# Scores in back-to-back pairs behind the first output tile, in four chunks of a fused attention and feed-forward kernel

## The chip, the cores and the metric

The kernel runs on one core of a Trainium2 chip. The core has a tensor engine (PE, with PEld for its weight loads), a vector engine (DVE), a scalar engine (ACT), a general engine (POOL) and a queue engine (SP); each works through its own list of instructions in order, and they wait for one another by semaphores. Matmuls write to PSUM, which has eight banks of 512 float32 per partition. The metric is the device time of one execution in microseconds; less is better.

## The reference

Attention with a decay bias, and behind it a gated feed-forward layer on the normalised result. There are 8 sequences, 8 heads, 576 positions and head size 64, so 4608 tokens of width 512; the feed-forward width is 1536.

```python
scores = scale * np.matmul(q, k.transpose(0, 1, 3, 2))
bias = -(cum[:, :, :, None] - cum[:, :, None, :])          # cum: running sum of max(s, 0)
scores = np.where(causal, -1e9, scores + np.minimum(bias, 0.0))
attn = softmax(scores); x = attn @ v                        # to (4608, 512)
xn = x / sqrt(mean(x * x) + 1e-6) * rms_g
g = xn @ w_gate; val = xn @ w_val
out = (g * sigmoid(g) * val) @ w_out
```

## The kernel before

The kernel computes for each block of 128 queries only the scores with its own key block and the one before it (the decay makes the rest vanish), and checks at the end that this and its other shortcuts were allowed; a general version stands behind a flag.

**The feed-forward layer sets the frame.** It runs over nine chunks of 512 tokens, numbered 0 to 8 (`ffn`, L660). In a chunk, twelve blocks of 128 hidden columns each take four matmuls for the gate (`Gp`, L670) and four for the value (`Vp`, L679), all 512 columns wide. ACT makes `T` (tanh) from `Gp` (L673), DVE makes `U` from `T` and `Gp` (L682) and then `Ht` from `U` and `Vp` (L675, the last one L687). After that come four output tiles, each of twelve matmuls into one bank `Op` (L692); ACT copies each bank to `osb` (L697) and a DMA writes it out.

**Attention is threaded into gaps.** After each group of four matmuls `step()` (L599) is called: 36 places in a chunk, which the code counts as `phase()` 1 to 36. Places 1 to 24 lie in the gate and value part, 25 to 27 in the first output tile (27 after its copy), 28 to 30 in the second, 31 to 33 in the third, 34 to 36 in the fourth. At a place a planner, run while the program is written, decides what else is issued: casts, loads, transposes by DMA, and either one **score run** or one **attention-value step**.

- A score run `s_step(b, kb, g)` (L225) is for sequence b, key block kb and four heads (g is 0 or 1; for kb 4 all eight heads). It has four matmuls of 64 rows and 256 columns (eight of 64 columns for kb 4), in pairs that use the two halves of the array at once, one for each parity of the head. Even heads go to one bank, odd ones to another. The pair of banks is `psS`, of which there is one. ACT then takes the exponentials to `E` (L274), half of them in the same place and the other half, through `pending`, at the start of the next place; POOL masks `E` (L283). `E` has eight slots, and each is free again when two attention-value steps have read it.
- An attention-value step `av_step(b, qb, g)` (L292) has eight matmuls of 65 columns (four for qb 0). DVE divides (`rZ` L313, `x_sb` L315). With g = 1 ACT also takes the sum of squares (`Square`, L321), POOL makes the normaliser `al_all` (L328, L331), and three places later DVE scales (L338) and a DMA transposes into `xnT`, from which the gate and value matmuls read.
- `can_s()` (L542) decides whether a score run may go: at least 2, 3 or 4 places after the last one, by how far it is from its due place; a free slot of `E`; its transposed keys and queries in place for five places. `can_av()` (L561) wants the scores five places old.

**Banks.** Four banks with the tag F (`psF()`, L101) serve `Gp`, `Vp` and `Op` in turn. In the compiled kernel a new tile takes the free bank whose last tile was finished with first, where "finished" means that its last reader stands earlier in the program. In the prologue some score runs already use two banks of this kind (`pairF()`, L812).

**Checks on DVE.** At places 25 to 35 DVE also runs `check_mag` (L369) and `check_max` (L375) over the cast keys and queries of later sequences: three rounds of one and two of these in chunk 3 (places 25 to 27, 29 to 31, 33 to 35) and three in chunk 4, where the last sequence is reached.

Of the kernel before, what the change touches and what calls it, by code (L numbers as in the profile page):

```python
# [26 lines left out]
def kernel(  # L27
# [13 lines left out]
    B, H, S, D = q.shape  # L41
# [39 lines left out]
    kqTn = kqT.rearrange("d a w (h n) -> d a w h n", h=HP)  # L81
    kqTx = kqT.rearrange("d a w (c h n) -> d a w c h n", c=NSC, h=HP)
    XB = 2
    KB = 4
    v_sb = mp.tile([128, 2, NSC, H, NV], BF16, name="v_sb")

    NE = 8
# [13 lines left out]
    def psF():  # L101
        return pp.tile([128, DM], FP32, name="psF", tag="F", bufs=4)
# [91 lines left out]
    def tail_step(b):  # L194
        pT = psT()
        nw = 2 if b < XB else 1
        for w in range(nw):
# [14 lines left out]
    eread = {}  # L212
    ecount = [0]
# [8 lines left out]
    def slot_free():  # L222
        return eread.get(ecount[0] % NE, 0) == 0

    def s_step(b, kb, g, pair=None):  # L225

        p = b % 2
        N = (256, 256, 256, 192, 64)[kb]
        W = 64 if kb == 4 else 256
        nj = 4 if kb == 4 else 2  # L230
        e = take_slot((b, kb, g), 2 if kb in (0, 1, 2, 3) else 2)
        if pair is None:
            ps = psS()
            pair = (ps[:, 0, :], ps[:, 1, :])
        heads = []
        for j in range(nj):
            hp = (0 if kb == 4 else 2 * g) + j
            for par in (0, 1):
                rs = slice(par * 64, par * 64 + 64)
                if b < KB:  # L240
                    kT = kqTn[rs, p, 0, hp, kb * 128:kb * 128 + 128]
                else:
                    kT = kqTx[rs, p, 0, kb, hp, :]
                if b < XB:
                    qT = kqTn[rs, p, 1, hp, kb * 128:kb * 128 + N]
                    M = N
                else:
                    qT = kqTx[rs, p, 1, kb, hp, 0:64] if kb == 4 else kqTx[rs, p, 1, kb:kb + 2, hp, :]
                    M = W
                nc.tensor.matmul(  # L250
                    pair[par][:, j * W:j * W + M], lhsT=kT, rhs=qT,
                    start=(j == 0), stop=(j == nj - 1))
                heads.append((2 * hp + par, par, j * W))
        if kb == 4:
            Ev = E[:, e].rearrange("p h (a n) -> p (h a) n", n=128)
            h0, nh, nq = 0, 8, 64
        else:
            Ev = E[:, e]
            h0, nh, nq = 4 * g, 4, 128

        def exps(part):
            for h, par, o in part:
                bh = b * H + h
                parts = [(0, N)]
                if b >= XB and kb == 3:
                    parts = [(0, 128), (128, 192)]
                for n0, n1 in parts:
                    eo = Ev[:, h - h0, n0:n1]
                    ei = pair[par][:, o + n0:o + n1]
                    if b >= XB and (n1 - n0) % 128 == 0:  # L270

                        eo = eo.rearrange("k (a p r) -> k a p r", p=32, r=4)
                        ei = ei.rearrange("k (a r p) -> k a p r", p=32, r=4)
                    nc.scalar.activation(out=eo, in_=ei, func=AF.Exp, scale=0.125,  # L274
                                         bias=biasK[:, kb, bh:bh + 1])

        def second(masked=True):
            exps(heads[nj:])
            if masked:
                mask()  # L280

        def mask():
            nc.gpsimd.affine_select(  # L283
                out=Ev[:, :, 0:nq], in_=Ev[:, :, 0:nq],
                pattern=[[0, nh], [1, nq]], compare_op=ALU.is_ge, fill=0.0, base=0,
                channel_multiplier=-1)

        exps(heads[:nj])
        second.mask = mask
        return second  # L290

# [81 lines left out]
    def check_max(i):  # L373
# [19 lines left out]
    pending = []  # L393
# [3 lines left out]
    def at(*key):  # L397
        return done.get(key, 10 ** 6)
# [19 lines left out]
    def check(b, ws=(1, 0)):  # L418
        t = slot[0] + (8 if b >= KB else 0)

        def when(w):
            if b < 2:
                return slot[0] % 2 and chunk[0] == b
            return phase() >= 25 and slot[0] >= t and (w == 0 or ready(0, "cast", b, 1))
        dve_side.extend((lambda w=w: when(w), f) for w in (ws if b < KB else (0, 1)) for f in (
            lambda w=w: check_mag(b, w), lambda: check_max(0), lambda: check_max(1),
            lambda w=w: done.__setitem__(("check", b, w), slot[0])))

    def phase():

        return slot[0] - first[0]
# [14 lines left out]
    def casts(b):  # L446
# [54 lines left out]
        done["T", b, hp, w] = slot[0]  # L501
        last["T"] = slot[0]

    def do_s(key, pair=None):
        b, kb, g = key
        second = s_step(b, kb, g, pair)
        done["S", b, kb, g] = slot[0]
        if kb == 4:
            done["S", b, 4, 1] = slot[0]
        last["S"] = slot[0]  # L510
        return second
# [30 lines left out]
    def can_s():  # L542
        if not s_seq or not slot_free():
            return False
        b, kb, g = s_seq[0]
        if b == 1 and (phase() < 24 and phase() % 2 == 0 or kb == 4 and at("AV", 1, 3, 1) > slot[0]):
            return False
        due = SLOTS * ((b * S + kb * 128) // DM) - (26 if b == 1 else 18 if b < 4 else 14)
        if slot[0] - last["S"] < (4 if slot[0] < due - 24 else 3 if slot[0] < due else 2):
            return False  # L550
        if b >= XB:
# [47 lines left out]
    def step(bare=False):  # L599

        slot[0] += 1
        while pending:
            pending.pop(0)()
        moved = False
        if scaled[0] < len(x_list):
            b, qb = x_list[scaled[0]]
# [10 lines left out]
        if not moved and x_seq and slot[0] - last["X"] >= 2 and not (  # L617
                scaled[0] < len(x_list) and ready(1, "AV", *x_list[scaled[0]], 1)):
            b, w, c = x_seq[0]
# [11 lines left out]
            run_side(pool_side)  # L631
        run_side(dve_side)
        if can_s():
            pending.append(do_s(s_seq.pop(0)))
            if t_seq and t_seq[0][0] == 1 and can_t():
                do_t(t_seq.pop(0))
            return
# [475 lines left out]
```

## Time and profile before

| what | value |
|---|---|
| median of 3 runs | 373.54 us (372.38 to 373.56) |
| the profiled execution's own time | 373.4 us |
| its span, first to last instruction | 371.5 us, granted clock 0.995 |
| busy: PE, DVE, ACT, POOL | 93%, 75%, 64%, 47% of the span |
| chunk 3, from first gate matmul to the next chunk's | 38.67 us (152.96 to 191.63) |
| chunk 4 | 37.57 us (191.63 to 229.20) |
| chunk 5 | 37.05 us (229.20 to 266.25) |
| chunk 6 | 36.06 us (266.25 to 302.31) |
| chunk 7, which holds no attention | 31.08 us (302.31 to 333.39) |

Busy time of PE is the sum of overlapping matmul spans, so the time that a group of matmuls takes is read from its start to the start of the next group. A few matmul records are missing from the trace (a group of four shows x3), and then the gap belongs to the missing one.

### The profile page before, as it was taken

How to read it: one execution, taken by the hardware profiler on the slowest of the kernel's cores; microseconds unless marked ns; L12 is line 12 of the kernel's file. 1: busy time of each engine (PE TensorE's matmuls, PEld its weight loads, DVE VectorE, ACT ScalarE, POOL GpSimd, SP SyncE). 2: the span in 40 equal slices, each digit the busy share in tenths (PEclk: the TensorE clock that was granted, in tenths of full speed). 3: DMA queues.
4: the chain of work that ended last, by engine and by line, in shares of the span. 5: the costliest groups of instructions: out<-in, count | busy, mean ns of one | idle time of the engine just before them, and what ended most of it. 6: DMA issues, size and time to landing. Idle time of an engine off the chain costs nothing.

```text
span 371.5 us, 6891 instructions
## 1 busy us (share of the span) xinstructions
PE 346.3 (93%) x2312; PEld 162.7 (44%) x2356; DVE 277.1 (75%) x523; ACT 238.7 (64%) x624; POOL 176.4 (47%) x281
## 2 busy tenths in 40 slices
PE   1888999899999999899999999999999999999992
PEld 1553444354444444444444444444444444444441
DVE  6777989499887878788889888885488558827820
ACT  3977687457977597777768776776777644223311
POOL 5968625966757474778837934533222300000000
PEclk9999999999999999999999999999999999999998
DMA  7999999999949499959969974993300230020011
GB/s 231 169 229 233 178 230 193 155 210 209 182 113 120 44 210 126 175 61 212 149 167 206 157 105 118 112 103 53 106 16 15 44 106 3 0 85 30 0 61 62
DMA packets 125627, 46.23 MB, mean 124 GB/s; under 512 B 104912, under 2 KB 120784, under 8 KB 125584
## 3 DMA queue, kind: packets, MB, share of 16 engines
q0 software_dynamic: 59920, 11.80, 42.9%
q1 hardware_dynamic: 53040, 24.33, 32.5%
q10 hardware_dynamic: 12624, 9.59, 10.4%
q8 instruction: 20, 0.33, 0.4%
q14 instruction: 23, 0.19, 0.2%
HBM read 38.16 MB, written 9.44 MB: 128 GB/s over the span
## 4 chain that ended last, share of the span: by engine, by line
PE 61%; DVE 14%; POOL 8%; issue 6%; DMA 5%; ACT 4%; ACTq 0%; POOLq 0%; DVEq 0%
PE psF L692 19%; PE psF L670 17%; PE psF L679 17%; PE psS L250 3%; DVE U L682 3%; DMA kq<-in_q_dram 3%; DVE Ht L675 2%; DVE x_sb L315 2%; POOL v_sb L175 2%; DVE xs_sb L338 2%; ACT E L274 2%; DVE acc L375 2%; POOL E L283 2%; DMA kq<-in_k_dram 1%; POOL kqn L141 1%
## 5 line engine op out<-in xcount | busy, mean ns | idle before, releaser
L274 ACT ACTIVATE E<-psS,biasK 128x256 bf16<-128x256 f32 (+3 forms) x352 | 115.1, 416 | 19.1 <-PE psS L250 18.0
L670 PE MATMUL psF<-xnT,wg_sb 128*128 128x512 bf16 x426 | 110.3, 379 | 2.6 <-DVE Ht L675 0.9
L679 PE MATMUL psF<-xnT,wv_sb 128*128 128x512 bf16 x408 | 109.3, 380 | 1.4
L692 PE MATMUL psF<-wout_sb,Ht 128*128 128x512 bf16 x419 | 100.5, 379 | 0.5 <-issue 0.2
L682 DVE SCALAR_TENSOR_TENSOR U<-T,psF 128x512 bf16<-128x512 f32 x108 | 73.7, 682 | 29.2 <-ACT T L673 29.0
L283 POOL TENSOR_SCALAR_AFFINE_SELECT E<-E 128x512 bf16<-128x512 bf16 x72 | 51.5, 716 | 85.5 <-ACT E L274 85.1
L673 ACT ACTIVATE T<-psF 128x512 f32<-128x512 f32 x108 | 64.6, 598 | 42.8 <-PE psF L670 37.5
L675 DVE TENSOR_TENSOR Ht<-U,psF 128x512 bf16<-128x512 bf16 x99 | 67.7, 683 | 6.6
L670 PEld LDWEIGHTS <-wg_sb 128*128 128x128 bf16 x432 | 38.8, 98 | 47.1 <-issue 8.0
L679 PEld LDWEIGHTS <-wv_sb 128*128 128x128 bf16 x432 | 38.6, 98 | 42.6 <-issue 4.6
L692 PEld LDWEIGHTS <-Ht 128*128 128x128 bf16 x432 | 38.7, 98 | 42.0 <-issue 2.3
L338 DVE SCALAR_TENSOR_TENSOR xs_sb<-x_sb,al_all,g_row 128x512 bf16<-128x512 bf16 (+1 forms) x40 | 31.9, 800 | 16.4 <-POOL al_all L331 14.8
L697 ACT ACTIVATE osb<-psF 128x512 f32<-128x512 f32 x36 | 21.4, 595 | 33.5 <-PE psF L692 30.5
L321 ACT ACTIVATE xs_sb<-x_sb 128x512 bf16<-128x512 bf16 (+1 forms) x36 | 23.0, 641 | 22.3 <-DVE x_sb L315 22.0
L175 POOL DMA_DIRECT2D v_sb<-in_v_dram x40 | 35.5, 888 | 0.3 <-issue 0.2
L375 DVE TENSOR_TENSOR acc<-acc,mag 128x1280 bf16<-128x1280 bf16 x32 | 29.0, 922 | 0.4
L250 PE MATMUL psS<-kqT 64*128 64x256 bf16 (+2 forms) x304 | 26.8, 262 | 1.7 <-ACT E L274 1.1
L306 PEld LDWEIGHTS <-E 128*128 128x128 bf16 x320 | 23.1, 101 | 11.3 <-POOL E L283 0.8
L328 POOL TENSOR_SCALAR al_all<-ss_all 128x1 f32<-128x1 f32 (+1 forms) x40 | 11.1, 278 | 29.8 <-ACT xs_sb L321 24.0
L300 PEld LDWEIGHTS <-E 128*128 128x128 bf16 x256 | 21.2, 101 | 8.1 <-DVE x_sb L315 0.7
L331 POOL TENSOR_TENSOR al_all<-al_all,mhalf 128x1 f32<-128x1 f32 (+1 forms) x40 | 22.3, 557 | 3.3
L141 POOL CAST kqn<-kq 128x512 bf16<-128x512 f32 (+1 forms) x30 | 20.7, 710 | 5.8 <-DMA kq<-in_k_dram 3.7
(94 smaller groups left out, 271.9 us busy)
## 6 DMA issues: line engine op xcount, KB each, us to landing
out_dram<-osb SPq DMA_DIRECT2D x36, 256.0 KB, 2.2
kq<-in_q_dram ACTq DMA_DIRECT2D x6, 1024.0 KB, 6.7
v_sb<-in_v_dram POOLq DMA_DIRECT2D x32, 128.0 KB, 6.0
kq<-in_k_dram ACTq DMA_DIRECT2D x2, 1024.0 KB, 9.3
kqn<-in_k_dram POOLq DMA_DIRECT2D x16, 128.0 KB, 4.8
wg_sb<-in_moe_w_gate_dram POOLq DMA_DIRECT2D x2, 768.0 KB, 10.1
wv_sb<-in_moe_w_val_dram POOLq DMA_DIRECT2D x2, 768.0 KB, 12.5
wout_sb<-in_moe_w_out_dram POOLq DMA_DIRECT2D x1, 1536.0 KB, 14.7
```

The lines of the kernel that those rows point to most:

```text
L175: nc.gpsimd.dma_start(out=v_sb[0:n, b % 2, c, :, 0:64], in_=v[b, :, c * 128:c * 128 + n, :].rearrange("h p d -> p h d"))
L250: nc.tensor.matmul(pair[par][:, j * W:j * W + M], lhsT=kT, rhs=qT, start=(j == 0), stop=(j == nj - 1))
L274: nc.scalar.activation(out=eo, in_=ei, func=AF.Exp, scale=0.125, bias=biasK[:, kb, bh:bh + 1])
L283: nc.gpsimd.affine_select(out=Ev[:, :, 0:nq], in_=Ev[:, :, 0:nq], pattern=[[0, nh], [1, nq]], compare_op=ALU.is_ge, fill=0.0, base=0, chan ...
L338: nc.vector.scalar_tensor_tensor(out=xs_sb[0:n, (b * NSC + qb) % NX, :], in0=x_sb[0:n, (b * NSC + qb) % NX, :], scalar=al_all[0:n, col:col ...
L375: nc.vector.tensor_tensor(out=acc[:, sl], in0=acc[:, sl], in1=mag[:, sl], op=ALU.max)
L670: nc.tensor.matmul(Gp, lhsT=wg_sb[:, cc, fs], rhs=xnT[:, cc, x0:x0 + DM], start=(cc == 0), stop=(cc == CC - 1))
L673: nc.scalar.activation(out=T, in_=Gp, func=AF.Tanh, scale=0.5)
L675: nc.vector.tensor_tensor(out=Ht[:, fb - 1, :], in0=pend[0], in1=pend[1], op=ALU.mult)
L679: nc.tensor.matmul(Vp, lhsT=wv_sb[:, cc, fs], rhs=xnT[:, cc, x0:x0 + DM], start=(cc == 0), stop=(cc == CC - 1))
L682: nc.vector.scalar_tensor_tensor(out=U, in0=T, scalar=1.0, in1=Gp, op0=ALU.add, op1=ALU.mult)
L692: nc.tensor.matmul(Op, lhsT=Ht[:, fb, tb * 128:(tb + 1) * 128], rhs=wout_sb[:, fb, :], start=(fb == 0), stop=(fb == FB - 1))
```

## The change

From chunk 3 on, at places 28 to 33, a score run may be followed at once, in the same place, by a second one. The first uses `psS` as always; the second takes two banks with the tag F and puts off its exponentials: the first half is issued two places later, the second half three places later (the first run's second half is issued one place later, as before). `pending` now holds pairs of a place and a function. In these chunks a single score run that is not within six places of its due place is held back at places 25 to 32, and in chunk 6 the last four score runs are held until they can go as pairs.

```diff
-    def s_step(b, kb, g, pair=None):
+    def s_step(b, kb, g, pair=None, hold=False):
...
-        exps(heads[:nj])
+        def head():
+            exps(heads[:nj])
+        if not hold:
+            head()
+        second.head = head
...
+        if b >= XB and slot[0] < due - HOLD and chunk[0] > 2 and 25 <= phase() <= 32 and not can_pair():
+            return False
+        if chunk[0] == B - 2 and len(s_seq) <= 4 and not can_pair():
+            return False
+        return s_ready(b, kb, g)
+
+    def can_pair():
+
+        if len(s_seq) < 2 or chunk[0] < 3 or not 28 <= phase() <= 33:
+            return False
+        return eread.get((ecount[0] + 1) % NE, 0) == 0 and s_ready(*s_seq[1])
...
-        while pending:
-            pending.pop(0)()
+        while pending and pending[0][0] <= slot[0]:
+            pending.pop(0)[1]()
...
         if can_s():
-            pending.append(do_s(s_seq.pop(0)))
+            pair = can_pair()
+            pending.append((slot[0] + 1, do_s(s_seq.pop(0))))
+            if pair:
+                b, kb, g = s_seq.pop(0)
+                more = do_s((b, kb, g), (psF(), psF()), True)
+                pending.extend([(slot[0] + 2, more.head), (slot[0] + 3, more)])
+                done["S", b, kb, g] = slot[0] + 2
+                last["S"] = slot[0] + 1
```

`XB` is 2, `HOLD` is 6 and `B` is 8. `s_ready` is the last part of the old `can_s`, unchanged.

More of the change, by code (lines that the diff above doesn't have):

```diff
@@ L83 @@
     XB = 2
+    HOLD = 6
     KB = 4
@@ L502, in do_t, with do_s @@
         last["T"] = slot[0]
-    def do_s(key, pair=None):
+    def do_s(key, pair=None, hold=False):
         b, kb, g = key
-        second = s_step(b, kb, g, pair)
+        second = s_step(b, kb, g, pair, hold)
         done["S", b, kb, g] = slot[0]
@@ L550, in can_s, with s_ready @@
             return False
+        if b >= XB and slot[0] < due - HOLD and chunk[0] > 2 and 25 <= phase() <= 32 and not can_pair():
[7 more added lines that the diff above has]
+        return eread.get((ecount[0] + 1) % NE, 0) == 0 and s_ready(*s_seq[1])
+    def s_ready(b, kb, g):
         if b >= XB:
@@ L633, in step @@
         if can_s():
-            pending.append(do_s(s_seq.pop(0)))
+            pair = can_pair()
[6 more added lines that the diff above has]
+                last["S"] = slot[0] + 1
+                if kb == 4:
+                    done["S", b, 4, 1] = slot[0] + 2
             if t_seq and t_seq[0][0] == 1 and can_t():
```

## The prediction

> **What bounds the kernel now.** First the busy line of the page, then the busy time by stretches, one for each of chunks 3 to 7:
>
> ```profile
> PE 346.3 (93%) x2312; PEld 162.7 (44%) x2356; DVE 277.1 (75%) x523; ACT 238.7 (64%) x624; POOL 176.4 (47%) x281
> ```
> ```profile
> 152.96:191.63 38.67, 37.65 (x264) 17.11 (x269) 31.64 (x58) 28.90 (x81) 28.30 (x44) 1.00 1.36 159
> 191.63:229.20 37.57, 37.31 (x265) 16.99 (x269) 33.55 (x65) 27.85 (x78) 22.29 (x36) 1.00 1.25 147
> 229.20:266.25 37.05, 36.79 (x252) 16.63 (x256) 25.67 (x53) 28.07 (x78) 15.16 (x27) 1.00 0.70 92
> 266.25:302.31 36.06, 35.80 (x240) 16.44 (x244) 24.29 (x48) 24.30 (x66) 9.30 (x18) 1.00 0.20 47
> 302.31:333.39 31.08, 30.92 (x142) 14.11 (x144) 20.71 (x35) 11.12 (x22) 0.00 (x0) 1.00 0.10 37
> ```
>
> PE (the second number) fills every chunk. Chunk 7 shows the bare feed-forward: 31.08 us for 144 matmuls, 0.216 each, 0.863 for four. What attention adds is read in the timeline of PE, from start to start:
>
> ```profile
> 181.16 2.75 PE L692 MATMUL psF<-wout_sb,Ht 128*128 128x512 bf16 x12
> 183.85 0.29 PE L250 MATMUL psS<-kqT 64*128 64x64 bf16 x8
> 184.07 1.04 PE L692 MATMUL psF<-wout_sb,Ht 128*128 128x512 bf16 x4
> ...
> 263.10 1.03 PE L692 MATMUL psF<-wout_sb,Ht 128*128 128x512 bf16 x4
> 264.06 0.39 PE L250 MATMUL psS<-kqT 64*128 64x256 bf16 x4
> 264.39 1.04 PE L692 MATMUL psF<-wout_sb,Ht 128*128 128x512 bf16 x4
> 265.26 0.29 PE L306 MATMUL psAV<-v_sb,E 128*128 128x65 bf16 x4
> 265.39 1.02 PE L692 MATMUL psF<-wout_sb,Ht 128*128 128x512 bf16 x4
> 266.25 1.03 PE L670 MATMUL psF<-xnT,wg_sb 128*128 128x512 bf16 x4
> ```
>
> Four matmuls ahead of another group take 0.86 (265.39 to 266.25), ahead of a score run 0.96; the run takes 0.33, the group after it 0.87. So a lone run costs 0.10 + 0.33 + 0.01 = 0.43 us; with 64 columns (kb 4) 0.10 + 0.22 + 0.01 = 0.33. An attention-value step costs 0.24, or 0.13 with four matmuls. Sums: chunk 6 is 31.08 + 6 × 0.43 + 0.33 + 8 × 0.24 + 0.13 = 36.04 against 36.06; chunk 5 comes out at 37.03 against 37.05. Chunk 4 has 0.2 over and chunk 3 has 1.0 over, which is waiting. From chunk 5 on no wait is left, only issue: what a run costs PE is what it costs the kernel.
>
> The 0.1 ahead of a run is visible in the waits as weight loads that cannot run ahead (0.42 each); the other two lines come up below:
>
> ```profile
> PEld L250 <- issue: 28.2, 67, 0.5
> ACT xs_sb L321 <- DVE x_sb L315: 22.0, 21, 2.0
> PE psS L250 <- ACT E L274: 1.1, 3, 0.5
> ```
>
> **The change, part by part.** I followed the planner's rules by hand from the places of before. Every chunk from 3 to 6 gets a pair at place 28 and one at 33: eight pairs. The 35 score runs of these chunks fall as 10, 11, 10, 4 instead of 10, 9, 9, 7. Chunks 0 to 2 don't change.
>
> *What a pair saves.* A second run with no full-height matmul ahead of it needs neither the 0.10 nor the tail. Three runs back to back stand in the prologue:
>
> ```profile
> 19.25 0.61 PE L250 MATMUL psF<-kqT 64*128 64x256 bf16 x4
> 19.64 0.53 PE L250 MATMUL psS<-kqT 64*128 64x192 bf16 x4
> 19.96 0.53 PE L250 MATMUL psF<-kqT 64*128 64x192 bf16 x4
> 20.43 0.40 PE L306 MATMUL psT<-v_sb,E 128*128 128x65 bf16 x4
> ```
>
> The middle one takes 0.32 for two steps of 192 columns, 1.2 columns per ns, at a stage where PE runs at half its later 2.37 columns per ns; nothing is lost between runs. At the later pace 256 columns twice make 0.22. So a second run costs 0.22 instead of 0.43, and for kb 4, with four steps of 0.03, 0.14 instead of 0.33: 6 × 0.21 + 2 × 0.19 = 1.64 us. Bounds: 0.1 a pair less if the second run still starts from empty weights; 0.22 a pair at most, since the columns must be streamed.
>
> In words of the Trainium skill (TensorEngine Tiling (Array Packing), Key Properties) changing the tiling mode drains the array, which would be the 0.10. Another of its pages (TensorE: Matmul & The Clock Gate, The mechanism) says that a weight load overlaps matmuls in flight only where its row group differs. By that each pair of score matmuls would wait for a load, and the second run would be hardly cheaper. By that the sum would be 374.3 (rival 3). The prologue rows speak against it.
>
> *What else goes.* The lone run at place 36 of chunk 3 waits for `psS` (eight matmuls take 1.98 before it at 189.31, not 1.82): 0.16 us, gone, since the pair at 33 takes it. The 0.55 wait of the run at 156.50 lies at place 3 of chunk 3, ahead of the change, and stays. Sum of savings: 1.8.
>
> *What is added: exponentials at the seam.* The number of exponentials is the same, but those of the pair at 33 meet the fourth output tile and the next chunk's first. ACT's order is: copy of tile 3, first run (two halves), the square of the attention-value step at 34, first half of the second run (35), copy of tile 4, second half (36), `T`. Four exponentials take 1.56, so a half 0.78; a copy 0.49 to the next start; a square 0.63. PE's order with the pair's start as 0: 0.55 the pair, 0.87, step at 34 (0.24), 0.86, 0.86 (fourth tile ends, 3.4), step at 36 (0.24), gate 0.86, value at 4.5. Banks: first in is first out by last reader, so the value group (`Vp`) of the next chunk takes the fourth tile's own bank, free when its copy ends; `Gp` and `Vp` of the next block take the pair's two banks. Before, no F bank waited for a score. So the path is the square, half a run, the copy.
>
> - Chunks 5 and 6 (DVE free there): the square starts 1.1 after its step (262.86 to 263.96), at 2.5; half a run to 3.9, copy ends 4.55. `Vp` wants the bank at 4.4: 0.12 each.
> - Chunk 4: the step at 34 has g = 0, no square; the copy ends 4.1: nothing. Here `U` is late next (the square of the step at 36 stands before `T`), about 0.3 us inside the need of the next gate.
> - Chunk 3: DVE runs its checks in front of the divide. Before:
>
> ```profile
> 187.91 0.17 DVE L313 RECIPROCAL rZ<-psT 128x4 f32<-128x4 f32 x1
> 188.12 0.42 DVE L315 TENSOR_TENSOR x_sb<-psT,rZ 128x256 bf16<-128x256 f32 x1
> ```
> ```profile
> 188.58 0.63 ACT L321 ACTIVATE xs_sb<-x_sb 128x512 bf16<-128x512 bf16 x1 [2.01 <-DVE x_sb L315]
> 189.21 0.58 ACT L697 ACTIVATE osb<-psF 128x512 f32<-128x512 f32 x1
> 189.69 1.56 ACT L274 ACTIVATE E<-psS,biasK 128x256 bf16<-128x256 f32 x4
> 191.29 0.60 ACT L697 ACTIVATE osb<-psF 128x512 f32<-128x512 f32 x1
> ```
>
>   That step began on PE at 184.95, and its square came 3.6 later. Now it stands at 34. DVE has 9.1 us of work from 181.6 on (scale 0.7, three `mag` at 0.85 to 1.27, five `max` at 0.8 to 1.1, a divide), and then the step's own divide, 0.55, so the square starts at 191.2; the pair, by the same count of matmuls from 178.76, starts at 187.45, 3.7 earlier; half a run to 5.05, copy ends 5.7. `Vp` wants it at 4.9 (a score run at place 1 of chunk 4 lies before it): 0.8, between 0.25 (`max` at 0.8 throughout) and 1.2.
>
> Together 1.1, bounds 0.5 and 1.7. The runs' own banks are free in time: the pair at 28 needs only DVE's last `U` and `Ht`, the pair at 33 the exponentials of the first pair, done 0.7 us before (4.5 after its start, against 5.2).
>
> *What is moved at no cost.* Three attention-value steps go from chunk 6 to 7, the last to place 6, with their squares (ACT busy 36% there), divides, scales and their transposes on SP: `xnT` of the last tokens is issued at place 9 of chunk 7, needed at chunk 8, 27 places or 23 us later; without that cover each us would count. PE pays 3 × 0.24 there instead of in chunk 6. The mask of each second run comes on POOL two places later; its reader stands seven places behind, some 3 us of cover. In chunk 4 the loads of V and the transposes of sequence 6 on POOL and SP move by a place or two, and stand ten places ahead of their readers. Score runs at places 1 and 4 of chunk 4 meet a late ACT: `psS` would be free just when the second wants it (at 8.6), like the 0.5 us wait in the list; inside the bounds.
>
> **Sum.** 373.4 − 1.8 + 1.1 = 372.7 us, against the profiled execution's own 373.4 (0.14 below the median).
>
> **Rivals.**
> 1. *The seam is hidden.* If the squares or copies come 0.3 earlier, or `max` at its short row, only 0.3 is given back: 373.4 − 1.5 to − 1.8, some 371.8. For it: chunks 4 to 6 are within 0.15 of it. Against: chunk 3's DVE queue, 90% busy from 181 to 190.
> 2. *The seam costs more than the pairs save.* One mechanism: the square of place 34 holds ACT at the end of all four chunks as in chunk 3. 4 × 0.85 = 3.4: 375.0. It decides from 0.77 a seam. For it: squares came 2.3 (225.81 to 228.14) and 3.6 us after their steps in chunks 3 and 4. Against: in chunks 5 and 6 they came at 1.1, and chunk 4 has none there.
> 3. *The second run isn't cheaper.* Saving 0.16 alone, give-back 1.1: 374.3. Against: the prologue rows.
>
> The Trainium skill (TensorEngine Tiling (Array Packing), PSUM Bottleneck) also says that tiling speeds up the matmuls, not the evacuation of PSUM; that is rival 2 in kind, and chunk 3's rows bear it out, those of 5 and 6 not.
>
> **How the numbers follow.** Forecast 0.45, rival 1 0.27, rival 2 0.18, rival 3 0.06, others 0.04. A measurement of this kernel tells 0.3% (1.1 us) from no change: faster is under 372.4, slower over 374.7. The forecast's own range, 371.9 to 373.3 by its bounds, puts a third in faster: 0.15, and with rival 1's 0.26 faster is 0.41. Rival 2 gives slower 0.16, rivals 3 and others 0.03: 0.19. Same has 0.40. The range goes from 371.5 (all saved, 373.4 − 1.85) to 374.6 (rival 3's upper side) and leaves out rival 2.
>
> **What would show it.** Right: at eight places a row of L250 into `psS` followed by one into `psF` 0.22 to 0.24 later, and one of them per chunk followed by the feed-forward; chunks 5 and 6 (with 10 and 4 runs) free of waits but 0.1; the first value group of chunk 4 waiting some 0.8 on `osb`. Wrong: a gap of 0.1 or more between the two runs (rival 3), or a wait of L679 on `osb`, or of L670 on `E`, over 0.77 at each seam (rival 2). The forecast falls if the hand-followed places are wrong, above all if fewer than eight pairs form, or if a new wait shows inside a chunk, at the score runs of places 1 to 4.

## The result, and the profile after

The change makes the kernel slower: 377.37 us median of 4 runs (376.71 to 377.46), against 373.31 for the kernel before beside it, a ratio of 1.0113 (95% interval 1.0094 to 1.0131). The profiled execution took 377.41 us, its span 375.6. The forecast was 372.7 with a range to 374.6.

The busy line of the page after, and the busy time by stretches, one for each of chunks 3 to 7 (from, to, length; then busy time and instructions of PE, PEld, DVE, ACT and POOL; clock, DMA share, GB/s):

```profile
PE 346.1 (92%) x2312; PEld 164.0 (44%) x2356; DVE 278.7 (74%) x523; ACT 236.4 (63%) x624; POOL 176.6 (47%) x281
```
```profile
152.23:190.80 38.57, 37.43 (x263) 17.29 (x269) 32.47 (x57) 27.82 (x78) 27.24 (x43) 1.00 1.35 154
190.80:232.12 41.32, 38.02 (x281) 17.66 (x283) 34.07 (x66) 29.84 (x85) 25.87 (x39) 1.00 1.06 132
232.12:270.63 38.51, 37.28 (x268) 17.32 (x270) 26.92 (x56) 29.87 (x84) 15.82 (x28) 1.00 0.68 98
270.63:304.24 33.61, 33.12 (x199) 15.56 (x199) 19.53 (x34) 17.29 (x46) 4.01 (x9) 1.00 0.13 40
304.24:337.49 33.25, 32.41 (x171) 14.80 (x171) 23.51 (x45) 13.12 (x33) 2.68 (x6) 1.00 0.14 42
```

No engine's share of the span rose. What is new is the distance between a chunk's length and PE's busy time in it: 3.3 us in chunk 4, where it was 0.3, 1.2 in chunk 5 (before 0.3), 0.8 in chunk 7 (before 0.2). Chunks 3 to 7 take 185.26 us instead of 180.43.

Three places in the timeline of PE (start, duration, instruction; in brackets the idle time and its releaser): the pair at place 33 of chunk 3 with the seam behind it (the end of one chunk and the first groups of the next), and two waits inside chunk 4.

```profile
187.17 0.39 PE L251 MATMUL psS<-kqT 64*128 64x256 bf16 x4
187.40 0.38 PE L251 MATMUL psF<-kqT 64*128 64x256 bf16 x4
187.72 1.04 PE L719 MATMUL psF<-wout_sb,Ht 128*128 128x512 bf16 x4
...
191.76 0.39 PE L251 MATMUL psS<-kqT 64*128 64x256 bf16 x4
193.40 0.81 PE L706 MATMUL psF<-xnT,wv_sb 128*128 128x512 bf16 x3 [1.24 <-ACT osb L724]
...
211.26 0.20 PE L311 MATMUL psT<-v_sb,E 128*128 128x65 bf16 x1 [0.81 <-POOL E L284]
...
218.29 1.02 PE L706 MATMUL psF<-xnT,wv_sb 128*128 128x512 bf16 x4 [0.79 <-DVE Ht L702]
```

The second run starts 0.23 us after the first, and the output group 0.32 after that: the pair does what it was to do. The value group at 193.40 comes 1.64 after the score run, where 0.33 is normal. Measured like this, from start to start against the same step without a wait, the new waits are:

| where | waits for | us |
|---|---|---|
| chunk 3, first output tile | last `Ht` (DVE) | 0.36 |
| seam 3 to 4, first value group | copy `osb` (ACT) | 1.31 |
| chunk 4, attention-value step at place 17 | mask of `E` (POOL) | 0.97 |
| chunk 4, a value group about place 24 | `Ht` (DVE) | 0.95 |
| seam 4 to 5, first value group | copy `osb` (ACT) | 0.94 |
| chunk 5, a score run | exponentials (ACT) | 0.25 |
| chunk 6, a gate group | `U` (DVE) | 0.33 |
| seam 6 to 7, first value group | copy | 0.13 |
| chunk 7, three groups | `Ht`, `U`, `U` (DVE) | 1.10 |

That is 6.3 us, 2.4 at the seams and 4.0 inside the chunks. Less the 1.8 that the pairs and the lost wait at place 36 save, and with 0.1 more at place 3 of chunk 3 (0.74, before 0.62), it makes 4.7 of the 4.83 found. The span rose by less, 4.1 (375.6, before 371.5), since the stretch ahead of chunk 3 was 0.73 shorter in this execution. Most of that lies ahead of chunk 1, a stretch that takes 72.9 to 75.3 us in the traces here, and so the experiments are read by the lengths of chunks 3 to 7.

### The profile page after: what moved, and what is told of

The parts are those of the page before. It is cut to its first block, busy times and chain, and to the rows that moved or that the text cites. A ratio compares the mean times of both kernels' runs of the same rounds, so it can differ in the third digit from the quotient of the medians.

```text
span 375.6 us, 6882 instructions
## 1 busy us (share of the span) xinstructions
PE 346.1 (92%) x2312; PEld 164.0 (44%) x2356; DVE 278.7 (74%) x523; ACT 236.4 (63%) x624; POOL 176.6 (47%) x281
## 3 DMA queue, kind: packets, MB, share of 16 engines
q1 hardware_dynamic: 53040, 24.33, 31.9%
## 5 line engine op out<-in xcount | busy, mean ns | idle before, releaser
L275 ACT ACTIVATE E<-psS,biasK 128x256 bf16<-128x256 f32 (+3 forms) x308 | 100.7, 421 | 8.5 <-PE psS L251 7.3
L719 PE MATMUL psF<-wout_sb,Ht 128*128 128x512 bf16 x416 | 99.4, 379 | 1.2 <-issue 0.5
L284 POOL TENSOR_SCALAR_AFFINE_SELECT E<-E 128x512 bf16<-128x512 bf16 x72 | 53.0, 736 | 91.9 <-ACT E L275 90.8
L343 DVE SCALAR_TENSOR_TENSOR xs_sb<-x_sb,al_all,g_row 128x512 bf16<-128x512 bf16 (+1 forms) x40 | 32.6, 816 | 9.9 <-POOL al_all L336 8.3
L380 DVE TENSOR_TENSOR acc<-acc,mag 128x1280 bf16<-128x1280 bf16 x32 | 30.2, 958 | 0.3
L251 PE MATMUL psS<-kqT 64*128 64x256 bf16 (+2 forms) x264 | 23.9, 265 | 1.8 <-ACT E L275 1.4
L251 PEld LDWEIGHTS <-kqT 64*128 64x128 bf16 x320 | 11.1, 97 | 26.7 <-issue 24.3
```

The source lines that it names most:

```text
L251: nc.tensor.matmul(pair[par][:, j * W:j * W + M], lhsT=kT, rhs=qT, start=(j == 0), stop=(j == nj - 1))
L284: nc.gpsimd.affine_select(out=Ev[:, :, 0:nq], in_=Ev[:, :, 0:nq], pattern=[[0, nh], [1, nq]], compare_op=ALU.is_ge, fill=0.0, base=0, chan ...
L343: nc.vector.scalar_tensor_tensor(out=xs_sb[0:n, (b * NSC + qb) % NX, :], in0=x_sb[0:n, (b * NSC + qb) % NX, :], scalar=al_all[0:n, col:col ...
L380: nc.vector.tensor_tensor(out=acc[:, sl], in0=acc[:, sl], in1=mag[:, sl], op=ALU.max)
L719: nc.tensor.matmul(Op, lhsT=Ht[:, fb, tb * 128:(tb + 1) * 128], rhs=wout_sb[:, fb, :], start=(fb == 0), stop=(fb == FB - 1))
```

## The experiments

The lengths of the chunks, from first gate matmul to the next chunk's, in us:

| kernel | 3 | 4 | 5 | 6 | 7 |
|---|---|---|---|---|---|
| before | 38.67 | 37.57 | 37.05 | 36.06 | 31.08 |
| after | 38.57 | 41.32 | 38.52 | 33.60 | 33.26 |
| pairs of chunk 3 alone | 38.71 | 42.13 | 37.59 | 35.64 | 31.08 |
| of chunk 4 alone | 38.76 | 37.46 | 37.30 | 35.50 | 31.08 |
| of chunk 5 alone | 38.93 | 37.56 | 36.93 | 35.76 | 31.08 |
| of chunk 6 alone | 39.36 | 37.56 | 37.05 | 34.91 | 33.24 |
| chunk 3, pair at 28 alone | 38.48 | 39.44 | 37.05 | 36.06 | 31.08 |
| chunk 3, no score run at places 1, 2 of chunk 4 | 38.47 | 39.53 | 37.05 | 36.06 | 31.08 |
| chunk 3, without checks | 38.67 | 39.47 | 37.05 | 35.64 | 31.08 |
| chunk 3, loads of V earlier | 38.72 | 40.12 | 37.05 | 35.64 | 31.08 |
| the same, step of 13 at 15 | 38.82 | 40.39 | 37.32 | 35.64 | 31.08 |
| the same as the last but one, casts later | 38.67 | 40.38 | 37.59 | 35.64 | 31.08 |
| chunks 4 to 6, decay checks later | 39.21 | 37.44 | 37.31 | 34.31 | 33.17 |
| chunk 6, odd places in chunk 7 | 38.98 | 37.56 | 37.05 | 34.91 | 32.26 |
| chunks 4 to 6, odd places in chunk 7 | 39.39 | 37.45 | 37.31 | 34.32 | 31.94 |
| all pairs, three causes removed | 38.07 | 38.68 | 37.30 | 33.60 | 32.26 |
| the same, step of 13 at 15 | 38.68 | 38.83 | 37.30 | 33.60 | 32.26 |
| all pairs, casts later as well | 37.84 | 37.99 | 37.29 | 33.60 | 32.28 |

Chunk 3 is the one that varies between executions, by the waits that a score run meets at its place 3 (0 to 1.0 us) and, where no pair stands at 33, at place 36 (0 to 0.65); the kernels are compared by chunks 4 to 7.

### Which chunk's pairs cost

Four kernels, each with the pairs of one chunk alone, here chunk 4; for chunks 3 and 5 the list holds their number, and for chunk 6 the two lines with `B - 2` stay as well.

```diff
-        if b >= XB and slot[0] < due - HOLD and chunk[0] > 2 and 25 <= phase() <= 32 and not can_pair():
-            return False
-        if chunk[0] == B - 2 and len(s_seq) <= 4 and not can_pair():
+        if b >= XB and slot[0] < due - HOLD and chunk[0] in (4,) and 25 <= phase() <= 32 and not can_pair():
             return False
...
-        if len(s_seq) < 2 or chunk[0] < 3 or not 28 <= phase() <= 33:
+        if len(s_seq) < 2 or chunk[0] not in (4,) or not 28 <= phase() <= 33:
```

> Pairs and the hold in chunk 3 alone (places 28 and 33); later chunks take single runs again, four places apart, but two places earlier in chunk 4 than before. Theory Q (the loss is queues: ACT at the end of a chunk, POOL and DVE in chunk 4 because the attention places moved by two against casts and loads, and the decay checks in chunk 7): two pairs save 0.4, the last Ht in the first output tile costs 0.36, the seam to chunk 4 1.3, the POOL and DVE waits inside chunk 4 about 1.9: 3.2 us slower than before. Theory B (each pair keeps two of four F banks, and each chunk with pairs loses alike, a quarter of the 4.1): 1.0 slower, inside chunk 3 and its seam, and chunk 4 keeps its own time.

> Pairs and the hold in chunk 4 alone; chunk 3 and chunk 4 up to place 22 stand as before. Theory Q: two pairs save 0.4, the seam to chunk 5 costs 0.9, no wait inside chunk 4 before place 24: 0.5 us slower than before. Theory B: 1.0 slower.

> Pairs and the hold in chunk 5 alone, where DVE has no more checks of keys and queries. Theory Q: two pairs save 0.4, no seam: 0.4 us faster than before (chunk 5 or 6 shorter by that), at most 0.1 of it lost at the seam. Theory B: 1.0 slower.

> Pairs in chunk 6 alone, with the hold of the last four runs, which sends three attention-value steps into chunk 7 beside the decay checks. Theory Q: two pairs save 0.4, the seam to chunk 7 costs 0.1, chunk 7 loses 1.1 beyond the 0.7 that the three steps take there instead of in chunk 6: 0.8 us slower. Theory B: 1.0 slower, at the seam, and chunk 7 loses nothing inside.

Measured: chunk 3 alone 376.77 us, a ratio of 1.0094 (1.0072 to 1.0117); chunk 4 alone 0.9995 (0.9978 to 1.0011); chunk 5 alone 0.9992 (0.9979 to 1.0005); chunk 6 alone 1.0045 (1.0030 to 1.0061). Chunks 4 to 7 sum to 141.76 before and to 141.34 and 141.33 with the pairs of chunk 4 or 5: 0.42 and 0.43 less, two pairs at 0.21, with no new wait. This is read from one trace each; the medians cannot tell so little. So the pairs save what was forecast where nothing is in their way, and theory B, by which each chunk with pairs loses alike, falls; the seam of 0.9 that theory Q expected behind chunk 4 did not come either. The loss has two sources: the pairs of chunk 3, by what they do to chunk 4 (four waits of 1.20, 0.99, 0.95 and 1.06 there and 0.53 in chunk 5), and those of chunk 6, by what they do to chunk 7 (0.12, 0.28, 0.50 and 0.32). In chunks 4 to 7 the four kernels differ from the kernel before by +4.68, -0.42, -0.43 and +1.00, together +4.83, and the changed kernel by +4.94: the four nearly add up.

### The seam behind chunk 3

Three kernels with chunk 3's pairs: only the pair at place 28; both, with the first score run of chunk 4 held until place 3; and both, without DVE's checks of sequences 5 to 7 (that part is not computed). The edits are shown against the kernel with the pairs of chunk 3 alone.

```diff
-        if len(s_seq) < 2 or chunk[0] not in (3,) or not 28 <= phase() <= 33:
+        if len(s_seq) < 2 or chunk[0] not in (3,) or not 28 <= phase() <= 30:
```
```diff
+        if chunk[0] == 4 and phase() < 3:
+            return False
         return s_ready(b, kb, g)
```
```diff
-            lambda w=w: check_mag(b, w), lambda: check_max(0), lambda: check_max(1),
+            (lambda w=w: check_mag(b, w)) if b < 5 else (lambda: None), (lambda: check_max(0)) if b < 5 else (lambda: None), (lambda: check_max(1)) if b < 5 else (lambda: None),
```

> Chunk 3 alone, with the pair at place 28 but not the one at 33: the runs of sequence 5 go singly at 33 and 36, and chunk 4 keeps the places of before. Theory Q (seam, then POOL and DVE in chunk 4 at moved places): no wait for the fourth tile's copy and none inside chunk 4; left are one pair's 0.2 saved and the 0.36 wait for the last Ht: within 0.4 us of before, chunk 4 at 37.6. Theory H (the hold at place 25 and the pair at 28, by what they shift in ACT and DVE, already bring the loss): most of the 4.7 that chunks 3 to 7 of the run with both pairs lost is still there.

> Chunk 3 alone with both pairs, but no score run at places 1 and 2 of chunk 4, so that the runs of chunk 4 stand at 3, 6, 10, 14, ... as in the kernel before, while the loads of keys and the casts stay two places earlier and the loads of V two later than in it. Theory M (the waits of 1.0 and 0.95 inside chunk 4 come from the attention places that moved by two): they go; left are the seam, 1.2 to 1.7, and 0.36: 1.2 to 1.7 us slower than before. Theory L (they come from loads and casts that crowd POOL at places 9 to 17, wherever attention stands): they stay, 3 us slower or more.

> Chunk 3 alone with both pairs, and the check of keys and queries of sequences 5 to 7 on DVE left out (that part is not computed). Theory D (the seam is late because DVE's checks stand before the divide, which the square, and with it ACT's order, waits for): the wait of 1.2 at the first value group of chunk 4 falls under 0.3, and the 1.06 of the score run at the end of chunk 4 goes too; the two waits inside chunk 4 stay, about 1.9. Theory X (ACT has too many exponentials at the seam, whatever DVE does): the seam stays at 1.0 or more.

Measured: 1.0033 (1.0012 to 1.0053), 1.0058 (1.0038 to 1.0078) and 1.0030 (1.0015 to 1.0045). Without the pair at 33 the seam has no wait, but a score run at place 3 of chunk 4 waits 0.81 for the exponentials, and the mask is late by 0.95 all the same. Chunks 4 to 7 lose 1.87, where theory Q expected next to nothing and theory H most of the 4.7: the pair at 28 and the hold bring a part of the loss by themselves. With the score run held, the value group waits 1.62 instead of 1.20, since nothing stands ahead of it; but inside chunk 4 the wait for the mask is gone and that for `Ht` falls from 0.95 to 0.49. So these two waits hang on the places of attention's runs and steps, as theory M said, the one for `Ht` in part. Without the checks the seam closes, in the timeline of PE:

```profile
191.31 1.03 PE L695 MATMUL psF<-xnT,wg_sb 128*128 128x512 bf16 x4
192.27 0.39 PE L251 MATMUL psS<-kqT 64*128 64x256 bf16 x4
192.60 1.04 PE L704 MATMUL psF<-xnT,wv_sb 128*128 128x512 bf16 x4
```

The value group comes 0.33 after the run; the waits at the end of chunk 4 (1.06, 0.53) are gone as well. So the seam is DVE's checks ahead of the divide, which hold back the square on ACT, the exponentials and the copy behind it. The changed kernel shows this chain in the timelines of DVE and ACT:

```profile
188.83 0.83 DVE L374 TENSOR_SCALAR mag<-kqn 128x2560 uint16<-128x2560 uint16 x1
189.69 1.13 DVE L380 TENSOR_TENSOR acc<-acc,mag 128x1280 bf16<-128x1280 bf16 x1
190.74 0.17 DVE L318 RECIPROCAL rZ<-psT 128x4 f32<-128x4 f32 x1
190.95 0.42 DVE L320 TENSOR_TENSOR x_sb<-psT,rZ 128x256 bf16<-128x256 f32 x1
```
```profile
191.41 0.63 ACT L326 ACTIVATE xs_sb<-x_sb 128x512 bf16<-128x512 bf16 x1 [2.07 <-DVE x_sb L320]
191.94 0.19 ACT L326 ACTIVATION_READ_ACCUMULATOR xs_sb<-x_sb 128x1 f32 x1
...
192.04 0.82 ACT L275 ACTIVATE E<-psF,biasK 128x256 bf16<-128x256 f32 x2
192.75 0.59 ACT L724 ACTIVATE osb<-psF 128x512 f32<-128x512 f32 x1
```

The step began on PE at 188.59, its square 2.8 later. The two waits inside chunk 4 (0.68 for the mask, 0.95 for `Ht`) stay without the checks.

### The waits inside chunk 4

First, with the pairs of chunk 3 alone, the five loads of V that POOL issues, moved to places 5 to 13 (in the changed kernel 9 to 17, before 7 to 15).

```diff
-            (early if b else later)(v_side, 6 if b else 16, [
+            (early if b else later)(v_side, 3 if b == 4 else 6 if b else 16, [
```

> The pairs of chunk 3 alone, and the five loads of V of sequence 6 on POOL at places 5, 7, 9, 11 and 13 of chunk 4 instead of 9 to 17. In the run with chunk 3's pairs alone the attention-value step of place 17 waited 0.99 us for POOL's mask and the value group after it 0.95 for Ht (chunk 4 took 42.13 us). Theory of the crowded POOL: casts (0.6 us each), loads of V (0.9) and sums over partitions (0.75) fall together in places 11 to 15 and make the mask late. Then both waits go, together from 1.94 to under 0.5, and chunk 4 takes 40.5 to 40.8 us; the waits at its two seams (1.18 and 1.06) stay. Rival, the waits come from the exponentials, shifted late by the seam: they stay at 1.6 or more together, and chunk 4 stays at 41.8 to 42.3. Second rival, the crowd only moves to places 5 to 9, where the casts of the K rows start: a new wait of 0.5 or more ahead of place 12.

Measured: 1.0053 (1.0027 to 1.0080). The wait for `Ht` is gone. In the changed kernel DVE's scale waited for POOL's `al_all`, which stood behind a load (215.25 to 215.95), and the `Ht` that PE wanted stood behind the scale:

```profile
216.89 0.75 DVE L343 SCALAR_TENSOR_TENSOR xs_sb<-x_sb,al_all,g_row 128x512 bf16<-128x512 bf16 x1 [1.66 <-POOL al_all L336]
217.56 0.68 DVE L702 TENSOR_TENSOR Ht<-U,psF 128x512 bf16<-128x512 bf16 x1
```

With the loads out of the way it does not. The wait for the mask stays at 0.99. So the theory was right for one of the two. Chunk 4, at 40.12, is shorter than the 40.5 to 40.8 expected, since the 1.06 at its end is gone too.

Next, for the mask, two further kernels on top of this one: the attention-value step of place 13 put to 15, and the casts of sequence 7 put from places 11 to 15 to 14 to 18.

```diff
+        if chunk[0] == 4 and phase() in (13, 14):
+            return False
```
```diff
-        pool_side.extend((lambda w=w: ready(7, "raw", b, w) and free(w), f) for w, f in fns)
+        pool_side.extend((lambda w=w: ready(7, "raw", b, w) and free(w) and not (b == 7 and chunk[0] == 4 and phase() < 14), f)
+                         for w, f in fns)
```

> The pairs of chunk 3 alone, the loads of V at places 5 to 13, and in chunk 4 no attention-value step at place 13 (it goes to place 15). Without this the steps stand at 5, 7, 9, 11 and 13, five of them two places apart, where the kernel before has 7, 9, 11 and 15; the step of place 17 waited 0.99 us for POOL's mask. Theory of the full row: each step gives DVE a divide (0.55) and every second one a scale (0.75) in front of the next U, so that the divide ahead of the square of the step at 13 comes late, ACT waits for it 1.35 us, and with it the exponentials and the mask. Then the wait of place 17 falls from 0.99 to 0.0 to 0.3, and chunk 4 takes 39.1 to 39.5 us instead of 40.12. Rival, POOL's casts in front of the mask alone: the wait stays at 0.8 or more and chunk 4 at 39.9 to 40.2.

> The pairs of chunk 3 alone, loads of V at places 5 to 13, and the five casts of sequence 7 on POOL at places 14 to 18 instead of 11 to 15, so that the two that stood in front of the late mask (0.64 and 0.60 us) now stand behind it. The theory of the full row has fallen: with the step of place 13 moved to 15 the wait of place 17 stayed at 0.99. Theory of POOL's queue in front of the mask (POOL runs without a gap from place 5 to 17, and two casts, a sum over partitions and three loads lie between the mask before and this one): the mask comes 1.2 us earlier, the wait of 0.99 goes to under 0.1, and chunk 4 takes 39.0 to 39.3 us instead of 40.12, of which 1.2 is the seam. Rival, the mask then waits for the exponentials, made late on ACT: the wait stays at 0.4 or more.

Measured: with the step moved the wait stays at 0.99 (374.38 us, one run), and that theory falls: the square on ACT still waits 1.35 for its divide, and the last exponential ahead of the mask still ends 18.2 us after the chunk's start (18.1 without the move), so it is not the step of place 13 that makes it late. With the casts moved the wait is gone (376.8 us in one run, which is read by its chunks). So POOL's queue is what PE waits for. The timeline of POOL in the changed kernel ahead of the mask that PE waits for at place 17:

```profile
204.58 1.07 POOL L284 TENSOR_SCALAR_AFFINE_SELECT E<-E 128x512 bf16<-128x512 bf16 x1 [0.18 <-ACT E L275]
205.60 0.89 POOL L176 DMA_DIRECT2D v_sb<-in_v_dram  x1
206.49 0.69 POOL L156 DMA_DIRECT2D kqn<-in_k_dram  x1
207.17 0.89 POOL L176 DMA_DIRECT2D v_sb<-in_v_dram  x1
208.04 0.63 POOL L150 CAST kqn<-kq 128x512 bf16<-128x512 f32 x1
208.76 0.19 POOL L333 TENSOR_SCALAR al_all<-ss_all 128x1 f32<-128x1 f32 x1
209.03 0.56 POOL L336 TENSOR_TENSOR al_all<-al_all,mhalf 128x1 f32<-128x1 f32 x1
209.56 0.60 POOL L150 CAST kqn<-kq 128x512 bf16<-128x512 f32 x1
210.12 1.08 POOL L284 TENSOR_SCALAR_AFFINE_SELECT E<-E 128x512 bf16<-128x512 bf16 x1
```

From the load at 205.60 on POOL works without a gap of over 0.1 us; the last exponential that this mask needs ended at 209.0. In the kernel before, the same stretch, and the step on PE that reads the mask:

```profile
205.57 0.68 POOL L283 TENSOR_SCALAR_AFFINE_SELECT E<-E 128x512 bf16<-128x512 bf16 x1
...
210.70 0.66 POOL L283 TENSOR_SCALAR_AFFINE_SELECT E<-E 128x512 bf16<-128x512 bf16 x1
```
```profile
211.56 0.19 PE L300 MATMUL psT<-v_sb,E 128*128 128x65 bf16 x1
```

There the mask ended at 211.36, 0.20 us ahead of its reader: the cover of this mask (the time from the end of a result to the start of its reader) was 0.2, not microseconds. The exponentials have their part too: the last one ended 2.7 us after the start of its score run before, and 4.3 after it now. With the casts moved the mask begins right behind it (210.54, the exponential ended at 210.47) and still ends only 0.06 ahead of its reader; no run took this part away alone. And both masks take 0.4 longer now (1.07 and 1.08 instead of 0.68 and 0.66), 0.8 together; why, the last section says.

With the casts later chunk 4 is nevertheless 40.38 us, not 39.0 to 39.3, because the waits of 1.08 and 0.53 at its end, absent with the loads of V moved alone, are back. Two rows in each of the two kernels show what differs. With the loads of V alone, DVE and then POOL, and DVE's next check:

```profile
220.61 0.82 DVE L374 TENSOR_SCALAR mag<-kqn 128x2560 uint16<-128x2560 uint16 x1
...
224.83 0.82 DVE L374 TENSOR_SCALAR mag<-kqn 128x2560 uint16<-128x2560 uint16 x1
```
```profile
221.33 0.66 POOL L284 TENSOR_SCALAR_AFFINE_SELECT E<-E 128x512 bf16<-128x512 bf16 x1 [2.89 <-ACT E L275]
...
225.28 0.86 POOL L284 TENSOR_SCALAR_AFFINE_SELECT E<-E 128x512 bf16<-128x512 bf16 x1 [1.16 <-ACT E L275]
```

With the casts later as well:

```profile
221.17 1.31 DVE L374 TENSOR_SCALAR mag<-kqn 128x2560 uint16<-128x2560 uint16 x1
...
225.89 1.26 DVE L374 TENSOR_SCALAR mag<-kqn 128x2560 uint16<-128x2560 uint16 x1
```
```profile
221.15 0.66 POOL L284 TENSOR_SCALAR_AFFINE_SELECT E<-E 128x512 bf16<-128x512 bf16 x1 [3.01 <-ACT E L275]
...
225.81 0.66 POOL L284 TENSOR_SCALAR_AFFINE_SELECT E<-E 128x512 bf16<-128x512 bf16 x1 [0.62 <-ACT E L275]
```

Where the mask comes first by 0.02 or 0.08 us, the check takes 0.44 to 0.49 longer, twice; where the check comes first, it takes 0.82. The divide behind them is 0.85 later against the chunk's start, and the square waits 3.50 us for it instead of 1.98. The kernel with chunk 3's pairs and no other edit, which has both waits, shows the same: there the mask comes 0.02 and 0.08 ahead, and the checks take 1.31 and 1.26. No run changes this order and nothing else, so that it brings the two waits is argued from three traces.

### Chunk 7

With the pairs of chunks 4 to 6, the checks of the decay, which share DVE with the steps there, were put behind place 16. Then, with the pairs of chunk 6 alone, the three attention-value steps that end up in chunk 7 were put to the odd places 3, 5 and 7 instead of 2, 4 and 6.

```diff
-        dve_side.extend((lambda: chunk[0] == B - 1 and slot[0] % 2, f) for f in [
+        dve_side.extend((lambda: chunk[0] == B - 1 and phase() > 16 and slot[0] % 2, f) for f in [
```
```diff
+        if chunk[0] == B - 1 and phase() % 2 == 0:
+            return False
```

> Pairs in chunks 4, 5 and 6 but not in 3, and the decay checks of chunk 7 moved from its first places to those after 16. By theory Q six pairs save 1.2, the seams cost 0.1 to 0.3 together and chunk 7 loses nothing beyond the three steps that it takes over: chunks 4 to 7 make 140.8 us instead of 141.8, and the whole is 0.9 us faster than before. If the decay checks were not what the steps in chunk 7 met, its 1.2 stay, and the time is that of before.

> The pairs of chunk 6 alone; in chunk 7 the three attention-value steps stand at odd places, behind a gate group, and not at 2, 4 and 6. Theory of the ring: at an even place the transfer T of the next block stands behind the square on ACT, the square behind the divide on DVE, the divide behind U, and U behind T, so that each step adds a wait; at an odd place T is ahead of the square. Then chunk 7 takes 31.08 + 3 x 0.24 + 0.1 (the seam) = 31.9 us, instead of 33.24 with the steps at even places, and the sum of chunks 3 to 7 falls by 1.3. Rival, any attention-value step in chunk 7 costs a wait, as its DVE is short of time: chunk 7 stays at 32.9 to 33.4.

Measured: with the decay checks moved chunk 7 stays at 33.17 (1.0039; 1.0009 to 1.0068): they are not the cause. At odd places it falls from 33.24 to 32.26, and the kernel from 1.0045 to 0.9991 (0.9970 to 1.0012), with one wait of 0.29 left; the forecast was 31.9. That wait goes when the checks of the decay stand behind place 16 as well: 31.94 in the first kernel of the next section. This points to 0.3 us for them at odd places; that kernel has the pairs of chunks 4 and 5 too. The ring (engines that wait for one another in turn) is to be seen in the first of the two kernels, where the decay checks are out of the way, in the timelines of ACT, DVE and PE:

```profile
310.03 0.63 ACT L326 ACTIVATE xs_sb<-x_sb 64x512 bf16<-64x512 bf16 x1 [2.66 <-DVE x_sb L320]
...
310.66 1.05 ACT L700 ACTIVATE T<-psF 128x512 f32<-128x512 f32 x2
```
```profile
311.26 0.69 DVE L709 SCALAR_TENSOR_TENSOR U<-T,psF 128x512 bf16<-128x512 f32 x1 [0.67 <-ACT T L700]
```
```profile
312.00 1.02 PE L697 MATMUL psF<-xnT,wg_sb 128*128 128x512 bf16 x4 [0.34 <-DVE U L709]
```

At an even place, behind a value group, the next block's `T` stands behind the square on ACT; the square waits for the divide, and DVE's `U` for `T`. At an odd place `T` stands ahead of the square, as ACT's timeline of the second kernel shows:

```profile
307.67 0.60 ACT L702 ACTIVATE T<-psF 128x512 f32<-128x512 f32 x1 [0.25 <-PE psF L699]
309.97 0.63 ACT L326 ACTIVATE xs_sb<-x_sb 64x512 bf16<-64x512 bf16 x1 [1.71 <-DVE x_sb L320]
```

Before, the steps with a square in the gate and value part of chunks 4 to 6 all stood at odd places. In the changed kernel the 0.33 in chunk 6 follows two steps at its places 2 and 4, with the same order on ACT (the square at 274.00, `T` at 274.63); no run put these at odd places.

### All together

The pairs of chunks 4 to 6 with both edits of chunk 7; the whole change with the causes found so far removed (checks left out, loads of V earlier, odd places); this with the step of place 13 moved; and this with the casts later instead.

> Pairs in chunks 4, 5 and 6, none in chunk 3; in chunk 7 the attention-value steps at odd places and the checks of the decay after place 16. By the theory (chunk 3's pair and chunk 7's even places are the whole loss) chunks 4 and 5 keep 37.4 and 37.3, chunk 6 takes 33.9 to 34.3 and chunk 7 31.9: 140.5 to 140.9 us against 141.76 in the kernel before, so 0.9 to 1.3 us faster, a ratio of 0.9965 to 0.9976. Rival, the ring also stands at odd places: chunk 7 at 33.2, and the kernel no faster than before.

> The whole change, with the three suspected causes taken away at once: the checks of sequences 5 to 7 on DVE (the three of the magnitude and the maximum) are left out, so that part isn't computed; the loads of V of sequence 6 stand at places 5 to 13 of chunk 4; the attention-value steps of chunk 7 stand at odd places. If these causes are all, chunks 3 to 7 take 179.0 to 180.0 us, against 180.43 before and 185.27 with the change as it stands, and the kernel is 0.4 to 1.4 us faster than before. If something else costs as well, the sum stays above 181.5 and the kernel is slower than before.

> The whole change with the three causes taken away as before (the checks of sequences 5 to 7 on DVE left out, so that part isn't computed; the loads of V at places 5 to 13; odd places in chunk 7) and no attention-value step at place 13 of chunk 4. By the theory of the full row the 0.68 us wait left in chunk 4 falls under 0.2 and chunk 4 takes 38.0 to 38.2 us instead of 38.68: all of chunk 4's loss is then accounted for. By the rival it stays at 38.6 to 38.8.

> The whole change with all causes taken away: the checks of sequences 5 to 7 on DVE left out (not computed), loads of V at places 5 to 13, casts of sequence 7 at places 14 to 18, odd places in chunk 7. By the theory of POOL's queue the 0.68 us left in chunk 4 goes, chunk 4 takes 38.0 to 38.1 us (48 score matmuls and 88 attention-value matmuls with nothing waiting), chunks 3 to 7 take 179.0 to 179.8 us, and the kernel is 0.6 to 1.4 us faster than before, a ratio of 0.996 to 0.9985. By the rival chunk 4 stays at 38.4 to 38.7.

Measured: the first takes 372.20 us, 0.9972 (0.9959 to 0.9984): a version that computes everything and beats both kernels, with a ratio as forecast; its chunks 4 to 7 sum to 141.0, just over the 140.5 to 140.9 forecast, against 141.76 before. The second: 0.9987 (0.9971 to 1.0003), chunks 3 to 7 at 179.9 as forecast, 0.68 left for the mask. The third keeps that wait at 0.67. The fourth: 0.9952 (0.9935 to 0.9969), with chunk 4 as PE's work alone, by the stretches 3 to 5 of this kernel:

```profile
153.83:191.66 37.83, 37.62 (x268) 17.18 (x269) 24.39 (x49) 28.62 (x82) 26.95 (x44) 1.00 1.37 154
191.66:229.65 37.99, 37.99 (x286) 17.52 (x283) 27.81 (x57) 30.31 (x85) 24.18 (x39) 1.00 1.31 151
229.65:266.94 37.29, 37.29 (x273) 17.21 (x271) 24.82 (x51) 28.56 (x80) 14.96 (x27) 1.00 0.66 93
```

Chunk 4 takes 37.99, 3.33 less than in the changed kernel, with no wait left. Chunks 3 to 7 sum to 179.0, 1.43 under the kernel before, with 1.1 of waits still in them (0.36, 0.33, 0.13, 0.30). Of the 1.43, 0.83 is chunk 3, whose wait at place 3 is absent in this execution; chunks 4 to 7 sum to 141.16, 0.60 under the kernel before. This kernel lacks the checks, which the kernel before has, and the kernel before was not run without them. So it is no version to use, and the 0.60 is no clean measure of the pairs; it shows that the loss goes when these causes are taken away.

## Why the prediction was wrong

- **The pairs** (places 28 and 33 of chunks 3 to 6, runs 10, 11, 10, 4): right.
- **What a pair saves:** right. The second run starts 0.23 us after the first in all eight pairs, and two pairs save 0.42 and 0.43 where they stand alone. Rival 3 falls, and with it the rule on weight loads that the prediction set beside it: in the pair at 187.17 the second run's first weight loads begin at 187.40, while the first run's last matmuls (187.29 to 187.56) are in flight. On this kernel a second run costs its columns. The 0.16 at place 36 went too.
- **The seams:** mechanism right, size off. Forecast 0.8, 0, 0.12, 0.12 (1.04, entered as 1.1); measured 1.31, 0.94, 0, 0.13. At chunk 3 the value group wanted its bank 4.92 us after the pair's start, as counted (4.9), but the square came at 4.24 instead of 3.7 and the copy ended at 6.17 instead of 5.7. DVE's work ahead of the divide took 9.8 us where 9.1 was counted (the scale 1.23 for 0.7, and three of the maxima 1.13, 1.19 and 1.27, above the counted 0.8 to 1.1), so that the step's own divide began when counted (190.7) although the scale began 0.6 earlier, while the pair stood 0.3 earlier than counted. At chunk 4 the forecast was 0, and the pairs of chunk 4 alone do give 0: the 0.94 comes with chunk 3's pairs, and a wait at the same end (1.06 there) goes when DVE's checks are left out. Rival 2 named the mechanism, but all seams together cost 2.4, not 3.4, and it does not account for the time.
- **"What is moved at no cost":** this is the step that failed. It priced at nothing the moves of chunk 4 and chunk 7, beyond the PE time of the three steps. They cost 0.97 + 0.95 and 1.10, and with 0.25 in chunk 5 and 0.33 in chunk 6 come to 3.6 us, twice what the pairs save. Each of its covers was wrong in the same way: it was measured as places between a result and its reader, not as the idle time of the queue that makes the result. "Its reader stands seven places behind" is true of the paired runs' masks, but a lone run's mask in chunk 4 had 0.20 us in hand before, with POOL full. The loads of V had ten places to their reader, but stand in POOL's queue ahead of masks and sums. And the three steps in chunk 7 were costed as PE time, ACT being busy 36%, although the order on ACT, not its share, sets the ring.
- **Not counted at all:** the score run that the hold takes from place 25 had covered the last `Ht` ahead of the first output tile; without it PE waits 0.36 in chunk 3.

## What to carry to other kernels

Moving work within an in-order schedule is priced on each queue that it passes: look in the trace for the time between the end of a result and the start of its reader there, since a full queue may leave a cover of tenths of a microsecond however many places lie between, as POOL's did here (0.2). Where steps of different engines alternate, ask behind which half a step lands, for the order may close a ring at one place and not at the next. Test a change that stands in several stages one stage at a time: here two of the four were free and the other two made the loss.

## What was unexpected of the hardware

POOL's mask takes 0.63 to 0.68 us alone, or beside DVE's `Ht`, `U` and divide; in the changed kernel all twelve masks that took over 1.0 us (1.04 to 1.83) overlap DVE's scale (L343) or a check (L374, L380). It works both ways: the check took 0.82 when it came first and 1.31 when the mask did. The Trainium skill (SBUF — State Buffer, Who interferes with whom) says that a vector instruction with two SBUF inputs, or in a two-port mode, shuts POOL out and the reverse, by which was issued first; the trace agrees, since the scale and the maximum read two tensors in SBUF, while `Ht` and `U` read one there and one in PSUM and leave the mask at 0.63. Of the check L374, which reads one tensor, no run here shows the mode. So two engines that wait for nothing of each other's set each other's durations, and which of them came first by a few hundredths of a microsecond went with 1.6 us of waits at the end of chunk 4 (1.08 and 0.53).
